# Attention decode over 16 heads: K and V loaded by pairs of heads, one head per 64 partitions, instead of head by head

## The chip, the core and the metric

The kernel runs on one NeuronCore of a Trainium2 chip. TensorE (PE) multiplies matrices into PSUM; VectorE (DVE), ScalarE (ACT) and GpSimdE (POOL) work element by element on SBUF, which has 128 partitions; the SyncE queue (SP) issues transfers, which 16 DMA engines carry out. Each engine runs its own program in order, and the programs meet only at semaphores. The metric is the device time of one execution in microseconds (us).

## The reference

One query per head against 8192 keys, with 16 heads of 256 numbers, in bf16:

```python
B, H, Sq, Sk, D = 1, 16, 1, 8192, 256
def reference(q, k, v):
    scale = q.shape[-1] ** -0.5
    scores = jnp.einsum("bhqd,bhkd->bhqk", q, k) * scale
    p = _softmax(scores, axis=-1)
    return jnp.einsum("bhqk,bhkd->bhqd", p, v)
```

K and V have 4 MB for each head, 134 MB together, and each byte is used once.

## The kernel before

**Layout.** A head's K lies on all 128 partitions: partition p holds the 64 keys 64p to 64p + 63 one behind the other, a row of 32 KB that is one contiguous run in memory. V lies alike. Two K buffers and two V buffers are used in turn.

**Loads.** SP issues all loads in the order of L16, 39 in all: the first head's K, the last head's K and the last three heads' V are cut (L15). K of head h waits until both engines that read K are through with head h - 2 (L121, L122), V of head h until the matmuls of head h - 2 are (L124). A transfer goes into its queue when its wait is over, behind those already there.

**Scores.** q of the head is copied to all partitions by a matmul into `qrow` (qcast, L244); ACT copies it to `q_now` in SBUF (q_copy, L347). A column is one key per partition. POOL multiplies the first 24 columns, four at a time, with `q_now` into one of two `prod` buffers (L184), and ACT sums each column into S (L396). DVE does the other 40 columns in four chunks of ten, product and sum in one instruction (L210). When all are in, DVE takes the maximum of each partition (m, L227).

**Softmax.** PE turns m into a row (L328), DVE takes its maximum (xmax, L199), PE spreads it over the partitions (L313), ACT negates it (L356) and makes the exponentials E and their sums (expo, L354). For head h this runs within the scores of head h + 1: xmax after DVE's first chunk, expo after ACT's second group.

**Output.** P·V is 32 matmuls, each on two columns with weights of 64 columns (doubles, L263); `collect` (L368) copies the two accumulators to SBUF, `gather` (L287) adds their parts up by four matmuls with selecting weights, `final` (L372) divides by the sum. PE's loop runs over h = 0 to 17, two rounds behind the scores. The last head's columns from 28 on go one by one, two matmuls each, straight to the output row (L330 to L342), so that only four columns are left when the last piece of V lands.

Of the kernel before, what the change touches and what calls it, by code (L numbers as in the profile page):

```python
# [5 lines left out]
ALU = mybir.AluOpType  # L6
# [4 lines left out]

NPL = 24
# [7 lines left out]
ROWS = 97  # L20
WIDE = BLK + 1
AHEAD = {"k1": 16, "kb": 16, "sp": 2, "pr": 1, "cm": 2, "pv": 1, "fin": 3, "rc": 3, "ex": 1, "mT": 1, "g": 1, "nb": 1}
STREAM_AHEAD = ("v0", "v1", "v0_40", "v1_48")


def bass_standalone__mha_softmax__decode_kernel(nc: bass.Bass, q: bass.AP, k: bass.AP, v: bass.AP, out: bass.AP):
# [15 lines left out]


    stream = []

    def load(kind, h):
        cuts = CUTS.get(f"{kind}{h}", (0,)) + (J,)
        for n, (a, b) in enumerate(zip(cuts, cuts[1:])):
            name = "kb" if kind == "k" and n else f"{kind}{h % 2}" + (f"_{a}" if n else "")
            stream.append((kind, h, a, b, name))  # L50

    for name in ORDER.split():
        load(name[0], int(name[1:]))

    with contextlib.ExitStack() as ctx:
# [16 lines left out]
        def back(h, n):  # L72

            if isinstance(h, int):
                return h - n
            return nc.s_assert_within(h - n, 0, H - 1, skip_runtime_bounds_check_because="the branch keeps it in range")
# [6 lines left out]
        S = sb("S", [P, H * J], FP32)  # L83
        E = sb("E", [P, 2 * EW], BF16)
        comb = sb("comb", [ROWS, 2 * D], FP32)
        sel = sb("sel", [ROWS, 2], FP32)
        m = sb("m", [P, 1], FP32)
        g = sb("g", [1, 1], FP32)
        negb = sb("negb", [P, 1], FP32)
        lsum = sb("lsum", [P, 1], FP32)  # L90
        recip = sb("recip", [WIDE, H], FP32)
        ident = sb("ident", [P, P], FP32)
        identb = sb("identb", [P, P], BF16)
        ones_row = sb("ones_row", [1, P], FP32)
        ones_col = sb("ones_col", [P, 1], FP32)
        o_all = sb("o_all", [1, H * D], out.dtype)

        acc = ps("acc", [P, 2 * D])
        ob = ps("ob", [P, 512])
# [6 lines left out]
        for name in ("pool", "cb", "cf", "ldq", "qp", "qb", "tp", "sp", "kd", "m", "mT", "g", "bc", "nb", "ex"):  # L106
            sem(name)
        for name in ("rc", "pr", "cm", "pv", "fin", "o"):
            sem(name)
        for _, _, _, _, name in stream:  # L110
            sem(name)

        def src(t, h):
            return t[0, h].rearrange("(p j) d -> p (j d)", p=P)

        @(lambda f: f(nc.sync))
        def _(sp):
            for kind, h, a, b, name in stream:
                if h >= 2 and a == 0:
                    if kind == "k":  # L120
                        sp.wait_ge(sem("kd"), (h - 1) * NC)  # L121
                        sp.wait_ge(sem("tp"), (h - 1) * NG)  # L122
                    else:
                        sp.wait_ge(sem("pr"), h + 2)  # L124
                buf = kbuf[:, h % 2 * J * D :] if kind == "k" else vbuf[h % 2]
                sp.dma_start(buf[:, a * D : b * D], src(k if kind == "k" else v, h)[:, a * D : b * D]).then_inc(  # L126
                    sem(name), 16
                )
            sp.wait_ge(sem(stream[-1][-1]), 16)
            sp.wait_ge(sem("fin"), LAST + 3)  # L130
            flat = out.rearrange("b h s d -> (b s) h d")
            rows = o_all[:, :].rearrange("s (h d) -> s h d", d=D)
            sp.dma_start(flat[:, 0:LAST, :], rows[:, 0:LAST, :]).then_inc(sem("o"), 16)
            sp.wait_ge(sem("fin"), H + 4)
            sp.dma_start(flat[:, LAST:H, :], rows[:, LAST:H, :]).then_inc(sem("o"), 16)
            sp.wait_ge(sem("o"), 32)
            sp.nop()
# [5 lines left out]

        @(lambda f: f(nc.gpsimd))
        def _(pool):
            def step(ins, n):
                ins.then_inc(sem("pool"), 1)
                pool.wait_ge(sem("pool"), n)

            def eye(t, n, done):  # L150
                step(pool.memset(t[:, :], 0.0), n)
                pool.affine_select(
                    out=t[:, :],
                    in_=t[:, :],
                    compare_op=ALU.not_equal,
                    fill=1.0,
                    base=0,
                    pattern=[[-1, P]],
                    channel_multiplier=1,
                ).then_inc(sem(done), 1)  # L160

            for name, n in AHEAD.items():
                pool.nop().then_inc(sem(name), n)
            for name in STREAM_AHEAD:
                pool.nop().then_inc(sem(name), 16)
            eye(identb, 1, "cb")
            eye(ident, 2, "cf")
            pool.memset(ones_row[:, :], 1.0).then_inc(sem("cf"), 1)
            pool.memset(ones_col[:, :], 1.0).then_inc(sem("cf"), 1)
            pool.memset(lsum[:, :], 0.0).then_inc(sem("cf"), 1)  # L170
            pool.memset(g[:, :], 0.0).then_inc(sem("cf"), 1)
            pool.memset(comb[:, :], 0.0).then_inc(sem("cf"), 1)
            step(pool.memset(sel[:, :], 0.0), 3)
            for n in range(4):
                step(pool.memset(sel[n * BLK : n * BLK + 1, n % 2 : n % 2 + 1], 1.0), n + 4)
            pool.memset(E[:, :], 0.0).then_inc(sem("cf"), 1)

            with pool.Fori(0, H) as h:
                par = pool.snap(h % 2)
                with pool.Fori(0, NG // 2) as i:  # L180
                    k_waits(pool, h)
                    for b in range(2):
                        pool.wait_ge(sem("sp"), h * NG + i * 2 + (b + 1))
                        pool.tensor_tensor(  # L184
                            out=prod[:, b * GRP * D : (b + 1) * GRP * D].rearrange("p (b d) -> p b d", b=GRP),
                            in0=kbuf[:, ds(par * (J * D) + i * (2 * GRP * D) + b * (GRP * D), GRP * D)].rearrange(
                                "p (b d) -> p b d", b=GRP
                            ),
                            in1=q_now[:, ds(par * D, D)].rearrange("p (b d) -> p b d", b=1).to_broadcast([P, GRP, D]),
                            op=ALU.mult,  # L190
                        ).then_inc(sem("tp"), 1)

        @(lambda f: f(nc.vector))
        def _(dve):
            def recips(h, n, after=0):
                dve.wait_ge(sem("pr"), h - n + (3 + after))
                dve.reciprocal(recip[:, ds(back(h, n), 1)], tot[0:WIDE, :]).then_inc(sem("rc"), 1)  # L197

            def xmax(h, n):  # L199
                dve.wait_ge(sem("mT"), h - n + 2)  # L200
                dve.tensor_reduce(g[:, :], mx[0:1, 0:P], AX.X, ALU.max).then_inc(sem("g"), 1)  # L201

            with dve.Fori(0, H) as h:
                par = dve.snap(h % 2)
                with dve.Fori(0, NC) as c:  # L205
                    k_waits(dve, h)
                    dve.wait_ge(sem("kb"), (h * 8 + c + 119) // 120 * 16 + 16)  # L207
                    for b in range(CH):
                        col = kbuf[:, ds(par * (J * D) + c * (CH * D) + (NPL + b) * D, D)]
                        ins = dve.scalar_tensor_tensor(  # L210
                            out=col,
                            in0=col,
                            scalar=SCALE,
                            in1=qrow[:, ds(par * 512, D)],
                            op0=ALU.mult,
                            op1=ALU.mult,
                            accum_out=S[:, ds(h * J + c * CH + (NPL + b), 1)],
                        )
                    ins.then_inc(sem("kd"), 1)
                    with dve.If(c == 0):  # L220
                        with dve.If(h > 1):
                            recips(h, 2)
                        with dve.If(h > 0):
                            xmax(h, 1)
# [18 lines left out]
        def _(pe):  # L243
# [19 lines left out]
            def doubles(par, a, b, waits):  # L263
                for j in range(a, b, 2):
                    if j in waits:
                        pe.wait_ge(*waits[j])
# [35 lines left out]
            for n in range(2):  # L302
                qcast(n, slice(n, n + 1))
# [142 lines left out]
```

## Time and profile before

| | |
|---|---|
| time, median of 3 runs | 318.48 us (318.28 to 318.66) |
| span of the profiled execution | 316.7 us |
| DVE busy | 232.5 us (73%) |
| POOL busy | 204.4 us (65%) |
| ACT busy | 197.9 us (62%) |
| PE busy | 141.7 us (45%), mean granted clock 0.752 |
| bytes read | 134.23 MB, 424 GB/s over the span |

The profile is one execution. The span runs from the first to the last instruction; the time has some 1.8 us more around it. Rows of the page's groups give line, engine, operation, output <- inputs, count, busy time and mean ns of one, then the engine's idle time just before and what ended most of it. Rows of the timeline give start and length in us, and idle time before in brackets with what released it. PEld is PE's loading of weights. An engine that is idle costs nothing by itself; what counts is which wait ends last.

### The profile page before, as it was taken

What the parts mean: (1) busy time and instruction counts of PE and PEld (TensorE: products, weight loads), DVE (VectorE), ACT (ScalarE), POOL (GpSimd) and SP (SyncE); (2) the same over time, 40 slices, a digit from 0 to 9 for tenths busy, and PEclk for the clock granted to TensorE, in tenths of its full rate; (3) what the DMA queues carried; (4) which work ended last, traced back from release to release, by engine and by line L of the source; (5) the groups of instructions that cost most, each with busy time, mean ns of one, the idle gap of its engine ahead of it and who ended that gap; (6) DMA issues with size and microseconds to landing.
All of it is one profiled execution on the core that took longest, in us unless ns stands there. A gap on an engine that the chain in (4) does not pass through costs nothing.

```text
span 316.7 us, 7915 instructions
## 1 busy us (share of the span) xinstructions
PE 141.7 (45%) x866; PEld 66.2 (21%) x866; DVE 232.5 (73%) x1329; ACT 197.9 (62%) x881; POOL 204.4 (65%) x115
## 2 busy tenths in 40 slices
PE   3101417253382642628282550715319064271977
PEld 1000103031130321204040220302113021130434
DVE  0797979497694967969797969769396793969800
ACT  2476737477374864768686857747386473968621
POOL 3788758395683857859687748568385783896500
PEclk9999999659576595857677595855857659585899
DMA  7999999999999999999999999999999999999996
GB/s 300 430 464 401 459 430 430 435 426 435 426 443 418 451 410 459 402 459 402 459 401 464 397 464 397 464 402 459 414 447 422 439 430 430 412 432 420 432 425 266
DMA packets 5653, 134.25 MB, mean 424 GB/s; under 512 B 642, under 2 KB 659, under 8 KB 916
## 3 DMA queue, kind: packets, MB, share of 16 engines
q1 hardware_dynamic: 5620, 134.23, 98.9%
q8 instruction: 1, 0.02, 0.0%
q10 hardware_dynamic: 32, 0.01, 0.0%
HBM read 134.23 MB, written 0.01 MB: 424 GB/s over the span
## 4 chain that ended last, share of the span: by engine, by line
DMA 59%; DVE 18%; issue 9%; DVEq 8%; PE 4%; SPq 0%; ACT 0%
DMA kbuf<-in_k_dram 35%; DMA vbuf<-in_v_dram 25%; DVE kbuf L210 18%; DVEq L210 5%; PE acc L268 4%; DVEq L207 1%; DVEq L205 1%; DVEq L142 1%; SPq L126 0%; PE ob L335 0%; DVEq L141 0%; DVE g L201 0%; DVE recip L197 0%; DVEq L225 0%; DVEq L197 0%
## 5 line engine op out<-in xcount | busy, mean ns | idle before, releaser
L210 DVE SCALAR_TENSOR_TENSOR kbuf<-kbuf,qrow x640 | 223.8, 417 | 52.6 <-issue 27.5
L184 POOL TENSOR_TENSOR prod<-kbuf,q_now 128x1024 f32 x96 | 201.9, 2124 | 90.1 <-DMA kbuf<-in_k_dram 59.0
L396 ACT ACTIVATE prod<-prod x384 | 154.5, 403 | 69.9 <-POOL prod L184 66.2
L268 PE MATMUL acc<-vbuf,E 128*64 128x512 bf16 x494 | 83.9, 513 | 30.7 <-DMA vbuf<-in_v_dram 30.1
L396 ACT ACTIVATION_READ_ACCUMULATOR prod<-prod x384 | 71.6, 186 | 0.0
L210 DVE DVE_READ_ACCUMULATOR kbuf<-kbuf,qrow x640 | 53.0, 83 | 0.0
L268 PEld LDWEIGHTS acc<-vbuf,E 128*64 128x64 bf16 x494 | 36.0, 146 | 72.3 <-issue 31.9
L313 PE MATMUL mx<-g,ones_row 1*128 1x1 f32 x34 | 9.7, 351 | 72.4 <-DVE g L201 72.3
L290 PE MATMUL ob<-comb,sel 97*1 97x128 f32 x144 | 14.2, 332 | 41.7 <-ACT comb L370 41.7
L350 ACT ACTIVATE q_now<-qrow (+1 forms) x17 | 6.5, 384 | 28.5 <-PE qrow L245 28.3
L313 PEld LDWEIGHTS mx<-g,ones_row 1*128 1x128 f32 x34 | 8.2, 298 | 76.9 <-DVE g L201 76.3
L279 PE MATMUL spare<-ident 128*128 128x512 f32 x36 | 22.2, 700 | 0.0
L290 PEld LDWEIGHTS ob<-comb,sel 97*1 97x1 f32 x144 | 5.6, 91 | 59.5 <-ACT comb L370 54.8
L328 PE MATMUL mx<-ident,m 128*1 128x128 f32 x32 | 8.1, 343 | 22.2 <-DVE m L227 22.2
L227 DVE TENSOR_REDUCE m<-S 128x1 f32 x16 | 3.5, 220 | 15.2 <-ACT prod L396 14.2
L370 ACT ACTIVATE comb<-acc 97x512 f32<-97x512 f32 x16 | 9.5, 596 | 6.1 <-PE tot L255 5.7
L359 ACT ACTIVATE E<-S,negb x16 | 9.3, 582 | 4.1 <-ACT negb L356 4.1
L377 ACT ACTIVATE o_all<-ob,recip 1x128 f32 x30 | 10.8, 359 | 1.5 <-PE ob L290 1.3
L197 DVE RECIPROCAL recip<-tot 33x1 f32 (+1 forms) x16 | 2.5, 155 | 10.2 <-PE tot L255 10.2
L328 PEld LDWEIGHTS mx<-ident,m 128*1 128x1 f32 x32 | 3.1, 100 | 24.6 <-DVE m L227 23.2
L245 PE MATMUL qrow<-q_sb,identb 16*128 16x256 bf16 x18 | 6.0, 347 | 4.7 <-DMA q_sb<-in_q_dram 4.7
L279 PEld LDWEIGHTS spare<-ident 128*128 128x128 f32 x36 | 5.8, 201 | 0.3
(27 smaller groups left out, 30.7 us busy)
## 6 DMA issues: line engine op xcount, KB each, us to landing
kbuf<-in_k_dram SPq DMA_DIRECT2D x14, 4096.0 KB, 21.1
vbuf<-in_v_dram SPq DMA_DIRECT2D x13, 4096.0 KB, 27.1
kbuf<-in_k_dram SPq DMA_DIRECT2D x2, 2176.0 KB, 13.3
kbuf<-in_k_dram SPq DMA_DIRECT2D x2, 1920.0 KB, 17.5
vbuf<-in_v_dram SPq DMA_DIRECT2D x1, 3072.0 KB, 29.9
vbuf<-in_v_dram SPq DMA_DIRECT2D x1, 2560.0 KB, 20.2
vbuf<-in_v_dram SPq DMA_DIRECT2D x1, 1792.0 KB, 11.1
vbuf<-in_v_dram SPq DMA_DIRECT2D x1, 1536.0 KB, 23.5
```

Of the source, the lines that this page charges most:

```text
L184: pool.tensor_tensor(out=prod[:, b * GRP * D : (b + 1) * GRP * D].rearrange("p (b d) -> p b d", b=GRP), in0=kbuf[:, ds(par * (J * D) + i * ...
L210: ins = dve.scalar_tensor_tensor(out=col, in0=col, scalar=SCALE, in1=qrow[:, ds(par * 512, D)], op0=ALU.mult, op1=ALU.mult, accum_out=S[:, ...
L268: ins = pe.matmul(acc[at : at + STRIP, :], lhsT=E[:, par * EW + j // 2 :][:, 0:STRIP], rhs=vbuf[par][:, j * D : (j + 2) * D], start=(j < 4 ...
L279: pe.matmul(spare[:, :].rearrange("p (b x) -> p b x", x=P), lhsT=ident[:, :], rhs=ident[:, :].rearrange("p (b x) -> p b x", b=1).to_broadc ...
L290: ins = pe.matmul(ob[row : row + 1, 0:HW], lhsT=sel[:, n : n + 1], rhs=comb[:, n * D + a : n * D + a + HW], start=(n == 0), stop=(n == 1), ...
L313: pe.matmul(sm, lhsT=ones_row[:, :], rhs=g[:, :], start=True, stop=True).then_inc(sem("bc"), 1)
L328: pe.matmul(mx[0:1, 0:P], lhsT=m[:, :], rhs=ident[:, :], start=True, stop=True).then_inc(sem("mT"), 1)
L350: act.activation(out=q_now[:, ds(par * D, D)], in_=qrow[:, ds(par * 512, D)], func=ACT.Copy).then_inc(sem("qb"), 1)
L359: act.activation(out=E[:, ds(i % 2 * EW, J)].rearrange("p (two x) -> p x two", two=2), in_=S[:, ds(i * J, J)].rearrange("p (x two) -> p x ...
L370: act.activation(out=comb[:, :], in_=acc[0:ROWS, :], func=ACT.Copy).then_inc(sem("cm"), 1)
L377: ins = act.activation(out=o_all[:, ds(i * D + a, HW)], in_=ob[row : row + 1, 0:HW], func=ACT.Copy, scale=recip[row : row + 1, ds(i, 1)],)
L396: ins = act.activation(out=part, in_=part, func=ACT.Copy, scale=SCALE, accum_out=S[:, ds(back(h, 0) * J + i * GRP + b, 1)],)
```

## The change

A load now brings K or V of two heads. Head 2n lies on partitions 0 to 63 and head 2n + 1 on partitions 64 to 127; a partition holds 128 keys, a run of 64 KB. There are eight pairs, 16 loads of 8 MB, five more by cuts, in all 21: only the last pair's K (two halves) and V (five pieces) are cut. There are two K buffers as before, of twice the size, but one V buffer; the last pair's V goes into the first K buffer. `q_now` is one buffer instead of two, and `q_copy` for the next pair comes after ACT's last group of this one. A pair has two sides of 64 columns; on each, POOL and ACT take 24 columns in groups of three (before: four) and DVE 40 in chunks of ten. Maximum, sum and result have two values, one for each head: `spread` makes two matmuls, `expo` two exponentials of 64 partitions each, interleaved with zeros in E so that one matmul serves both heads with different weights. `expo` comes after ACT's third group of the next pair, `collect` and `final` after its last. P·V runs in the round of the next pair; in the last round PE waits for the last pair's m before it starts the pair before. The last pair's columns from 92 on go one by one.

The diff, cut to its core:

```diff
-GRP = 4
+GRP = 3
-CUTS = {"k0": (0, 34), "k15": (0, 34), "v13": (0, 48), "v14": (0, 40), "v15": (0, 28, 48, 60)}
-ORDER = "k0 k1 v0 k2 v1 k3 v2 k4 v3 k5 v4 k6 k7 v5 k8 v6 k9 v7 k10 v8 k11 v9 k12 v10 k13 v11 k14 v12 k15 v13 v14 v15"
-LAST_PAIRED = 28
+SIDES = 2
+ORDER = "k0 k1 v0 k2 v1 k3 v2 k4 v3 k5 v4 k6 v5 k7 v6 v7"
+CUTS = {"k7": (0, 64), "v7": (0, 56, 92, 112, 124)}
+LAST_PAIRED = 92
...
+    NP = H // 2
+    HP = P // 2
+    J = Sk // HP
+    HJ = J // SIDES
...
+    NG = SIDES * NPL // GRP
+    SG = NPL // GRP
+    SC = (HJ - NPL) // CH
+    NC = SIDES * SC
...
-        vbuf = [sb(f"vbuf{i}", [P, J * D], dt) for i in range(2)]
-        q_sb = sb("q_sb", [H, D], dt)
-        q_now = sb("q_now", [P, 2 * D], dt)
+        vbuf = sb("vbuf", [P, J * D], dt)
+        q_now = sb("q_now", [P, D], dt)
...
+        def src(t, n):
+            return t[0, 2 * n : 2 * n + 2].rearrange("h (p j) d -> (h p) (j d)", p=HP)
...
+            for kind, n, a, b, name in stream:
+                if a == 0:
+                    if kind == "k" and n >= 2:
+                        sp.wait_ge(sem("kd"), (n - 1) * NC)
+                        sp.wait_ge(sem("tp"), (n - 1) * NG)
+                    elif kind == "v" and n == LAST:
+                        sp.wait_ge(sem("kd"), LAST * NC)
+                        sp.wait_ge(sem("tp"), LAST * NG)
+                    elif kind == "v" and n >= 1:
+                        sp.wait_ge(sem("pr"), n)
+                if kind == "k" and n == 1:
+                    sp.nop().then_inc(sem("k1"), 16)
+                    sp.nop().then_inc(sem("kb"), 16)
+                if kind == "k":
+                    buf = kbuf[:, n % 2 * J * D :]
+                else:
+                    buf = last_v if n == LAST else vbuf
+                sp.dma_start(buf[:, a * D : b * D], src(k if kind == "k" else v, n)[:, a * D : b * D]).then_inc(
                     sem(name), 16
                 )
...
+            with pool.Fori(0, NP) as h:
                 par = pool.snap(h % 2)
+                with pool.Fori(0, SIDES) as s:
+                    with pool.Fori(0, SG // 2) as i:
+                        k_waits(pool, h)
+                        side_wait(pool, h, s)
+                        for b in range(2):
+                            pool.wait_ge(sem("sp"), h * NG + s * SG + i * 2 + (b + 1))
+                            pool.tensor_tensor(
...
+            with dve.Fori(0, NP) as h:
                 par = dve.snap(h % 2)
+                with dve.Fori(0, SIDES) as s:
+                    with dve.Fori(0, SC) as c:
+                        k_waits(dve, h)
+                        side_wait(dve, h, s)
+                        for b in range(CH):
+                            col = kbuf[:, ds(par * (J * D) + s * (HJ * D) + c * (CH * D) + (NPL + b) * D, D)]
...
+                        ins.then_inc(sem("kd"), 1)
+                        with dve.If(c == 0):
+                            with dve.If(h > 0):
+                                with dve.If(s == 0):
+                                    xmax(h, 1)
+                                with dve.If(s == 1):
+                                    recips(h, 1)
...
+            def spread():
+                for n in range(2):
+                    ins = pe.matmul(
+                        sm[n * HP : (n + 1) * HP, :],
+                        lhsT=ones[0:1, :].to_broadcast([1, HP]),
+                        rhs=g[:, n : n + 1],
+                        start=True,
+                        stop=True,
+                    )
+                ins.then_inc(sem("bc"), 1)
...
+            with pe.Fori(0, NP) as h:
                 par = pe.snap(h % 2)
+                with pe.If(h > 0):
+                    pe.wait_ge(sem("g"), h)
+                    spread()
+                    pe.wait_ge(sem("ex"), h)
+                    total()
+                with pe.If(h == LAST):
+                    pe.wait_ge(sem("m"), NP)
+                    turned()
+                    pe.wait_ge(sem("g"), NP)
+                    spread()
+                with pe.If(h > 0):
+                    pe.wait_ge(sem("v"), h * 16)
+                    doubles(acc, 0, vbuf, 0, J).then_inc(sem("pr"), 1)
+                with pe.If(h < LAST):
+                    with pe.If(h > 0):
+                        keep_running()
+                        pe.wait_ge(sem("cm"), h)
+                        pe.wait_ge(sem("fin"), h)
+                        gather().then_inc(sem("pv"), 1)
                     pe.wait_ge(sem("m"), h + 1)
-                    pe.matmul(mx[0:1, 0:P], lhsT=m[:, :], rhs=ident[:, :], start=True, stop=True).then_inc(sem("mT"), 1)
-                    qcast(par, ds(h + 2, 1))
+                    turned()
+                    with pe.If(h < NP - 2):
+                        qcast(back(h, -2), par)
+            cuts = CUTS["v7"]
+            e = EW
+            pe.wait_ge(sem("ex"), NP)
+            total()
+            doubles(acc_last, e, last_v, 0, cuts[1], cuts, LAST_PAIRED)
+            pe.wait_ge(sem("cm"), LAST)
+            pe.wait_ge(sem("fin"), LAST)
+            gather().then_inc(sem("pv"), 1)
+            doubles(acc_last, e, last_v, cuts[1], LAST_PAIRED, cuts, LAST_PAIRED).then_inc(sem("pr"), 1)
+            keep_running()
+            pe.wait_ge(sem("cm"), NP)
+            pe.wait_ge(sem("fin"), NP)
+            gather()
...
+                    pe.wait_ge(sem(f"w{j}"), 16)
+                at = e + pos(j)
...
+            def q_copy(n, at):
+                act.wait_ge(sem("qp"), n + 1)
+                act.activation(out=q_now[:, :], in_=qrow[:, ds(at * 512, D)], func=ACT.Copy).then_inc(sem("qb"), 1)
...
+                at = EW if h is NP else 0
+                for x in range(2):
+                    rows = slice(x * HP, (x + 1) * HP)
+                    ins = act.activation(
+                        out=E[rows, at : at + 2 * J].rearrange(
+                            "p (b two i t) -> p b i two t", b=J // BLK, two=2, t=2
+                        )[:, :, :, :, x],
+                        in_=S[rows, ds(i % 2 * J, J)].rearrange("p (b i two) -> p b i two", b=J // BLK, two=2),
+                        func=ACT.Exp,
+                        bias=negb[rows, :],
+                        scale=1.0,
+                        accum_out=lsum[rows, :],
+                    )
+                ins.then_inc(sem("ex"), 1)
...
+            with act.Fori(0, NP) as h:
+                par = act.snap(h % 2)
+                other = act.snap((h + 1) % 2)
+                with act.Fori(0, SIDES) as s:
+                    with act.Fori(0, SG) as i:
+                        act.wait_ge(sem("tp"), h * NG + s * SG + i + 1)
...
                         with act.If(h > 0):
+                            with act.If(s == 0):
+                                with act.If(i == 2):
+                                    expo(h, 1)
+                with act.If(h < LAST):
+                    q_copy(h + 1, other)
+                    with act.If(h > 0):
+                        collect(h, 1, acc)
+                        final(h, 1)
+            expo(NP, 1)
+            collect(LAST, 1, acc)
+            final(LAST, 1)
+            collect(NP, 1, acc_last)
```

More of the change, by code (lines that the diff above doesn't have):

```diff
@@ L129, in _ @@
             sp.wait_ge(sem(stream[-1][-1]), 16)
+            sp.wait_ge(sem("fin"), LAST + 1)
+            flat = out.rearrange("b (n two) s d -> two (b n s) d", two=2)
+            rows = qo[:, :].rearrange("t (n d) -> t n d", d=D)
+            sp.dma_start(flat[:, 0:LAST, :], rows[:, 0:LAST, :]).then_inc(sem("o"), 16)
             sp.wait_ge(sem("fin"), LAST + 3)
[L131 to L135, printed above, removed]
+            sp.dma_start(flat[:, LAST:NP, :], rows[:, LAST:NP, :]).then_inc(sem("o"), 16)
             sp.wait_ge(sem("o"), 32)
@@ L172, in _ @@
[L172 to L178, printed above, removed]
-                par = pool.snap(h % 2)
[L180 to L191, printed above, removed]
+            step(pool.memset(ident[:, :], 0.0))
@@ new lines, in _ @@
+            keep(ident, 0, 1, -1, ALU.not_equal, 1.0)
+            step(pool.memset(ones, 1.0))
+            step(pool.memset(half[:, :], 1.0))
+            for c in (0, BLK):
+                step(pool.memset(half[HP:P, c : c + 1], 0.0))
+                step(pool.memset(half[0:HP, c + 1 : c + 2], 0.0))
+            step(pool.memset(E[:, :], 0.0))
+            for c in range(2):
+                step(
+                    pool.tensor_tensor(
+                        out=sel[:, 2 * c : 2 * c + 2],
+                        in0=ident[0:ROWS, c * BLK : c * BLK + 2],
+                        in1=ident[0:ROWS, STRIP + c * BLK : STRIP + c * BLK + 2],
+                        op=ALU.add,
+                    )
+                )
@@ L203, in _ @@
-            with dve.Fori(0, H) as h:
-                par = dve.snap(h % 2)
[L205 to L224, printed above, removed]
+                dve.wait_ge(sem("mT"), h - n + 1)
@@ L233, in _ @@
+            recips(NP, 1)
+            dve.wait_ge(sem("pv"), NP + 1)
+            dve.wait_ge(sem("rc"), NP)
             row, a = halves[1]
             dve.tensor_scalar(
-                out=o_all[:, LAST * D + a : LAST * D + a + HW],
-                in0=ob[row : row + 1, 0:HW],
-                scalar1=recip[0:1, LAST:H],
+                out=qo[:, LAST * D + a : LAST * D + a + HW],
+                in0=ob[row : row + 2, 0:HW],
+                scalar1=recip[row : row + 2, LAST:NP],
                 scalar2=None,
@@ L251, in qcast, with turned, total, doubles @@
                 ).then_inc(sem("qp"), 1)
-            def total(h):
-                pe.wait_ge(sem("ex"), (h * H + 2 * H + 1) // (H + 1))
+            def turned():
+                pe.matmul(mx[0:1, 0:P], lhsT=m[:, :], rhs=ident[:, :], start=True, stop=True).then_inc(sem("mT"), 1)
+            def spread():
[6 more added lines that the diff above has]
+                        stop=True,
+                    )
+                ins.then_inc(sem("bc"), 1)
+            def total():
                 pe.matmul(
-                    tot[0:WIDE, :],
-                    lhsT=lsum[:, :].to_broadcast([P, WIDE]),
-                    rhs=ones_col[:, :],
+                    tot[0 : BLK + 2, :],
+                    lhsT=half[:, :],
+                    rhs=lsum[:, :],
                     start=True,
                     stop=True,
-                ).then_inc(sem("pr"), 1)
-            def doubles(par, a, b, waits):
+                ).then_inc(sem("tt"), 1)
+            def doubles(to, e, buf, a, b, waits=(), last=J):
                 for j in range(a, b, 2):
                     if j in waits:
-                        pe.wait_ge(*waits[j])
+                        pe.wait_ge(sem(f"w{j}"), 16)
                     at = j // 2 % 2 * STRIP
+                    x = pos(j)
                     ins = pe.matmul(
-                        acc[at : at + STRIP, :],
-                        lhsT=E[:, par * EW + j // 2 :][:, 0:STRIP],
-                        rhs=vbuf[par][:, j * D : (j + 2) * D],
+                        to[at : at + STRIP, :],
+                        lhsT=E[:, e + x : e + x + STRIP],
+                        rhs=buf[:, j * D : (j + 2) * D],
                         start=(j < 4),
-                        stop=(j >= J - 4),
+                        stop=(j >= last - 4),
                         skip_group_check=True,
@@ L290, in gather @@
                         ins = pe.matmul(
[L291 to L292 removed]
+                            ob[row : row + 2, 0:HW],
+                            lhsT=sel[:, 2 * n : 2 * n + 2],
                             rhs=comb[:, n * D + a : n * D + a + HW],
@@ L342, in _ @@
                     )
[L343 removed]
+            ins.then_inc(sem("pv"), 2)
         @(lambda f: f(nc.scalar))
         def _(act):
[L347 to L352 removed]
+            def q_copy(n, at):
+                act.wait_ge(sem("qp"), n + 1)
+                act.activation(out=q_now[:, :], in_=qrow[:, ds(at * 512, D)], func=ACT.Copy).then_inc(sem("qb"), 1)
@@ L368, in collect @@
-            def collect(h, n):
-                act.wait_ge(sem("pr"), h - n + 4)
-                act.activation(out=comb[:, :], in_=acc[0:ROWS, :], func=ACT.Copy).then_inc(sem("cm"), 1)
+                at = EW if h is NP else 0
[10 more added lines that the diff above has]
+                        accum_out=lsum[rows, :],
+                    )
@@ L372, in final, with collect @@
+                ins.then_inc(sem("ex"), 1)
+            def collect(h, n, frm):
+                act.wait_ge(sem("pr"), h - n + 1)
+                act.activation(out=comb[:, :], in_=frm[0:ROWS, :], func=ACT.Copy).then_inc(sem("cm"), 1)
             def final(h, n):
-                act.wait_ge(sem("pv"), h - n + 4)
-                act.wait_ge(sem("rc"), h - n + 4)
+                act.wait_ge(sem("pv"), h - n + 1)
+                act.wait_ge(sem("rc"), h - n + 1)
                 i = back(h, n)
@@ L400, in _ @@
                                 scale=SCALE,
-                                accum_out=S[:, ds(back(h, 0) * J + i * GRP + b, 1)],
+                                accum_out=S[:, ds(par * J + s * HJ + i * GRP + b, 1)],
                             )
                         ins.then_inc(sem("sp"), 1)
-                    with act.If(i == 1):
                         with act.If(h > 0):
-                            with act.If(h < H + 1):
-                                expo(h, 1)
-                        with act.If(h > 2):
-                            final(h, 3)
-                with act.If(h > 1):
-                    collect(h, 2)
-            act.wait_ge(sem("pv"), H + 4)
-            act.wait_ge(sem("rc"), H + 3)
-            act.activation(out=o_all[:, LAST * D : LAST * D + HW], in_=ob[0:1, 0:HW], func=ACT.Copy, scale=recip[0:1, LAST:H]).then_inc(
+                            with act.If(s == 0):
[10 more added lines that the diff above has]
+            collect(NP, 1, acc_last)
+            act.wait_ge(sem("pv"), NP + 1)
+            act.wait_ge(sem("rc"), NP)
+            act.activation(out=qo[:, LAST * D : LAST * D + HW], in_=ob[0:2, 0:HW], func=ACT.Copy, scale=recip[0:2, LAST:NP]).then_inc(
                 sem("fin"), 1
```

230 lines of the change are left out of this document (94 added, 136 removed).

## The prediction, made before the changed kernel was timed

> **What bounds the kernel now.** I read the span, the DMA row and the costliest groups on the page first, then the busy time by windows, the PE timeline, and last the end of the timeline.
>
> ```profile
> span 316.7 us, 7915 instructions
> q1 hardware_dynamic: 5620, 134.23, 98.9%
> L210 DVE SCALAR_TENSOR_TENSOR kbuf<-kbuf,qrow x640 | 223.8, 417 | 52.6 <-issue 27.5
> L184 POOL TENSOR_TENSOR prod<-kbuf,q_now 128x1024 f32 x96 | 201.9, 2124 | 90.1 <-DMA kbuf<-in_k_dram 59.0
> ```
> ```profile
> 24.00:260.00 236.00, 105.19 (x581) 48.50 (x583) 187.12 (x1073) 155.02 (x702) 162.50 (x78) 0.71 1.00 432
> 294.00:313.00 19.00, 15.76 (x142) 7.71 (x138) 5.65 (x32) 7.18 (x26) 2.90 (x2) 0.95 1.01 427
> ```
>
> The 16 DMA engines are busy for 98.9% of 316.7, or 313 us; every compute engine idles in between. The loads are the bound, and only what the tail adds behind the last byte counts besides. The windows (span and length, then busy PE, PEld, DVE, ACT, POOL, the clock, DMA share, GB/s) show a full DMA share throughout: 432 GB/s with whole 32 KB rows and 427 where the last heads come in pieces of 2 to 20 KB. The stream has a steady beat, seen in PE's blocks of 32 paired matmuls (start, length), of which those from 236.57 to 275.43 were released by a landed V:
>
> ```profile
> 143.25 4.92 PE L268 MATMUL acc<-vbuf,E 128*64 128x512 bf16 x32 [0.17 <-issue]
> ...
> 236.57 6.04 PE L268 MATMUL acc<-vbuf,E 128*64 128x512 bf16 x32 [4.31 <-DMA vbuf<-in_v_dram]
> 256.00 6.56 PE L268 MATMUL acc<-vbuf,E 128*64 128x512 bf16 x32 [4.46 <-DMA vbuf<-in_v_dram]
> 275.43 5.39 PE L268 MATMUL acc<-vbuf,E 128*64 128x512 bf16 x32 [4.31 <-DMA vbuf<-in_v_dram]
> 301.24 2.35 PE L268 MATMUL acc<-vbuf,E 128*64 128x512 bf16 x20
> 309.09 1.70 PE L268 MATMUL acc<-vbuf,E 128*64 128x512 bf16 x14 [1.18 <-DMA vbuf<-in_v_dram]
> ```
>
> Two 4 MB loads take 19.43 us (236.57 to 256.00), which is one load of a pair. The end, in order:
>
> ```profile
> 299.21 0.22 DVE L227 TENSOR_REDUCE m<-S 128x1 f32 x1 [0.26 <-DVE kbuf L210]
> 311.09 0.60 ACT L370 ACTIVATE comb<-acc 97x512 f32<-97x512 f32 x1 [2.06 <-PE tot L255]
> 312.25 1.15 PEld L335 LDWEIGHTS ob<-vbuf,E 128*1 128x1 bf16 x40
> 314.06 1.06 PE L335 MATMUL ob<-vbuf,E 128*1 128x128 bf16 x32 [0.48 <-DMA vbuf<-in_v_dram]
> 315.16 0.36 ACT L414 ACTIVATE o_all<-ob,recip 1x128 bf16<-1x128 f32 x1 [3.47 <-PE ob L335]
> ```
>
> The last scores are complete at 299.2, 15 us before the last V columns arrive at 314.06, so the softmax and most of P·V hide under the stream. The span ends 1.5 us after L414 starts, and the time shown, 318.48, is 1.8 us more than the span.
>
> **The loads.** Bytes are the same, so long runs gain only what a row costs beside its bytes. From 427 to 432 is 1.2% between rows of about 10 KB (mean of the last pieces) and 32 KB. If that is a fixed cost per row, f/10 - f/32 = 1.2% gives f = 0.17 KB, and 64 KB instead of 32 KB saves 0.17/64 = 0.3%: 0.8 us over the stream, 0.6 by pair 6. Ends: nothing if the 64 KB row is cut in two, 1.2% (3.7 us) if the pieces' whole loss is repeated; I take 0.8, nearest to the row of whole loads. [...]
>
> **Do the buffers keep the stream full?** K of pair 0 lands after two 4 MB loads. V10 (in the order of L16 the 24th load of 4 MB) was seen at 236.57, so byte for byte K0 is there at 236.57 - 11 x 19.43 = 22.8, V0 at 61.7. Pair 0 takes DVE and POOL some 29 to 30 us (below), to 53; K2 has to be issued before V0 ends at 61.7: 8 us to spare. V_n needs the one V buffer: V5 is in at 256.0, its 64 matmuls take 9 (below), and V6's turn comes at 275.4: 10 us to spare. So the stream runs through; V7 has landed at about 313, as V15 does now.
>
> **What no longer hides: the scores.** K lies in units twice as long, whole until pair 7 (only k7 is cut), and the last 40 us of stream are V6 and V7. K6 is the 12th of 16 loads, so it lands when V10 does: 236.6 - 0.6 = 236.0. Then pairs 6 and 7 are scored, one behind the other.
>
> ```profile
> 266.42 4.20 POOL L184 TENSOR_TENSOR prod<-kbuf,q_now 128x1024 f32 x2 [5.45 <-DMA kbuf<-in_k_dram]
> 268.80 0.42 ACT L396 ACTIVATE prod<-prod  x1 [3.52 <-POOL prod L184]
> 270.98 4.20 POOL L184 TENSOR_TENSOR prod<-kbuf,q_now 128x1024 f32 x2 [0.36 <-issue]
> 284.46 0.39 ACT L350 ACTIVATE q_now<-qrow  x1 [1.34 <-PE qrow L245]
> 285.03 0.42 ACT L396 ACTIVATE prod<-prod  x1 [0.18 <-issue]
> 286.55 0.19 ACT L396 ACTIVATION_READ_ACCUMULATOR prod<-prod  x1
> 287.20 4.20 POOL L184 TENSOR_TENSOR prod<-kbuf,q_now 128x1024 f32 x2 [1.80 <-ACT prod L396]
> 288.84 0.17 ACT L356 ACTIVATE negb<-mx 128x1 f32<-128x1 f32 x1 [0.51 <-PE mx L313]
> 289.27 0.58 ACT L359 ACTIVATE E<-S,negb  x1 [0.26 <-ACT negb L356]
> 289.63 0.73 ACT L377 ACTIVATE o_all<-ob,recip 1x128 f32 x2
> ```
> ```profile
> 8.15 1.02 PE L290 MATMUL ob<-comb,sel 97*1 97x128 f32 x8
> ```
>
> POOL and ACT form a chain through two prod buffers. A POOL group of 4 columns takes 2.12; of 3 columns 1.6 (by size; it lies between 1.59 and the 2.12 of today). ACT starts 0.27 after POOL ends (266.42 + 2.12 to 268.80) and takes 1.7 for four columns (285.03 to 286.74), 1.3 for three. POOL needs 0.46 to see a freed buffer (286.74 to 287.20) and 0.36 for its loop. Two groups thus take 2 x 1.6 + 0.36 = 3.56 by POOL alone, 1.6 + 0.27 + 1.3 + 0.46 = 3.63 around a buffer: I take 3.6. A pair has 48 such columns, 16 groups, 8 rounds: 28.8, less the first 0.36, plus ACT's last 1.57.
>
> expo is now in ACT's path after the third group: 0.43 from negb to the exponential, then two of about 0.65 (the row's 0.58, with 64 more elements in each row): 1.8. ACT's later groups free POOL's buffers, so POOL stalls: group 2 is done at 6.7 from POOL's start, expo until 8.5, group 3 until 9.8, POOL goes on at 10.3 instead of 8.8: 1.5. **Pair 6** takes 28.8 - 0.36 + 1.57 + 1.5 = 31.5. POOL starts 0.7 after PE would see the landing (K14 fell midway between 256.00 and 275.43, at 265.7; POOL began at 266.42): 236.7 + 31.5 = 268.2.
>
> **Pair 7** can't start before: q_now is one buffer, and q_copy comes after ACT's last group. POOL starts 1.0 later (0.1 + 0.39 + 0.46). But behind q_copy ACT now runs collect (0.60), waits for gather, cold at 1.02, and runs final (0.73); then its loop jumps back, 1.34 before L350 today. ACT's first group starts 4.4 after the end of pair 6. The rounds follow: ACT's groups 0 and 1 end at 5.7 and 7.0, POOL's groups 2 and 3 at 7.8 and 9.4, ACT's group 2 at 9.4, expo at 11.3, ACT's group 3 at 12.6, POOL's groups 5 and 6 start at 13.1 and 15.1; five more rounds (18.0 - 0.36) and ACT's 1.57 make 34.3. The scores are complete at 268.2 + 34.3 = 302.5, and m starts 0.3 later: **302.8, against 299.2 now**. If the jumps of the new loop over sides cost like the one below, it is up to 3 us more; I take nothing, as POOL's 0.36 is nearest.
>
> DVE beside it:
>
> ```profile
> 16.58 0.33 DVE kbuf L210
> 20.18 0.33 DVE kbuf L210
> ```
> ```profile
> 170.04 0.22 DVE L227 TENSOR_REDUCE m<-S 128x1 f32 x1 [0.26 <-DVE kbuf L210]
> 171.79 0.42 DVE L210 SCALAR_TENSOR_TENSOR kbuf<-kbuf,qrow  x1 [1.53 <-issue]
> 266.72 0.42 DVE L210 SCALAR_TENSOR_TENSOR kbuf<-kbuf,qrow  x1 [3.41 <-issue]
> ```
>
> Ten columns repeat every 3.60 (16.58, 20.18): a pair is 28.8. Even if DVE alone set the pace, it starts at 236.0 + 1.0 (265.7 to 266.72), has two pairs of 28.8 with 2.0 between (m's wait 0.26 and 170.04 to 171.79), and m starts at 296.9. That is the floor.
>
> **The tail from m (M).** PE's order in its last round is: wait for pair 7's m, turned, spread, and only then pair 6's 64 matmuls, although V6 has been there since 294; V7's come behind them, and nothing hides any of it.
> - M to the first matmul: now 299.21 to 301.24, 2.0; with a second spread 2.1.
> - 64 matmuls: warm they cost (2.35 - 1.70)/6 = 0.108 each; blocks of 32 after idling took 4.92 to 6.56, 5.39 at 275.43, or 1.9 more than 32 x 0.108. 64 x 0.108 + 1.9 = 8.8; I take 9.0 (8.4 to 10). They end at M + 11.1.
> - total 0.4, 28 matmuls of V7 3.0, gather 0.45, 18 matmuls 1.9, drain 0.3: M + 17.2. V7 has landed by then. collect of pair 6 and final run beside this.
> - collect of pair 7 to the first single: 311.09 to 312.25 now, so M + 18.4. keep_running is beside it.
> - 72 singles at 1.15/40 = 0.029, and 0.2: M + 20.7. L414 and the end, 1.5: M + 22.2.
>
> 302.8 + 22.2 = 325.0, and 1.8 outside: **326.8, say 327**. [...]
>
> **The rivals.**
> - *Tail hidden (faster, 4%).* One point decides: M at or before 292. Then M + 22 falls on the last landing, the stream alone decides, and it gives 318.5 - 0.8 = 317.7. For it: 0.8 gained, DVE idle 52.6 today. Against it: two pairs would need 27.5 us each, and DVE's floor is 28.8. DVE's floor itself, M at 296.9, gives 296.9 + 22.2 + 1.8 = 320.9; that is the forecast's low end.
> - *The stream breaks (8%).* q is now read as rows of two partitions beside K0's long rows; if it, the late first K or the one V buffer costs more than the 8 to 10 us to spare, each further us moves everything: 330 to 340. Against it: the sums above.
> - *Slower rows (8%).* The pitch from partition to partition doubles to 64 KB. Were the rate 3% lower for it (two and a half times the largest difference between the windows), K6 would come 7 us later and M with it: 334. No row has any other pitch than 32 KB; the equal rates of whole and cut rows speak against it. [...]
> - *Not one run of 64 KB* but two of 32: inside the forecast, 0.6 to 0.8 us more.
>
> **How the numbers follow.** The forecast has 80%: 320.9 (DVE's floor) to 331 (3 us of jumps, 1 of cold matmuls). Beyond lie the two slow rivals; to leave out no more than 2 in 10 the range is 320.5 to 332, which loses the fast rival and most of the broken stream. A measurement tells 0.2% from no change: faster 4%, within 2%, slower 94%.
>
> **What would show it.** DMA share near full to about 313, with gaps only if a buffer was late; a rate of 432 to 434 GB/s; POOL groups at 1.6 and rounds at 3.6; m of the last pair at 302.8; V6's block of 64 starting 2 us after it and not at its landing at 294; then PE busy without a wait for DMA to 323. The forecast is wrong if m comes before 297, if the 64 run before m, or if DMA idles in the middle.

## The result, and the profile after

| | before | after |
|---|---|---|
| time, median | 318.56 us (318.28 to 318.66, 4 runs) | 326.57 us (324.94 to 326.67, 4 runs) |
| ratio after / before | | 1.0242, 95% interval 1.022 to 1.0264 |
| span of the profiled execution | 316.7 us | 325.3 us |

The changed kernel is 2.4% slower; the medians lie 8.0 us apart. (Of the kernel with rows of 32 KB further down, one run, 328.18 us at a granted clock of 0.623 against 0.731 to 0.748 of its others, is in a slower state and left out.) In what follows K6 is K of pair 6, V6 its V, and the singles are the 72 matmuls on one column each at the end. The page of its profile, the lines that answer to those of before:

```profile
span 325.3 us, 7432 instructions
...
q1 hardware_dynamic: 3044, 134.23, 95.7%
q8 instruction: 2, 0.03, 0.0%
...
L244 DVE SCALAR_TENSOR_TENSOR kbuf<-kbuf,qrow x640 | 223.8, 417 | 62.1 <-issue 56.1
L215 POOL TENSOR_TENSOR prod<-kbuf,q_now 128x768 f32<-128x768 bf16 x128 | 207.8, 1640 | 89.1 <-DMA kbuf<-in_k_dram 43.1
```

The packets are fewer (3044, of 5620) and longer. Their time is 95.7% of 325.3, or 311.3 us, against 313.2 before: the loads themselves got shorter. The span has grown past their end. Windows of after (span and length, busy PE, PEld, DVE, ACT, POOL, then clock, DMA share, GB/s):

```profile
24.00:260.00 236.00, 68.48 (x442) 30.86 (x444) 191.71 (x1095) 157.30 (x690) 174.29 (x108) 0.71 1.00 433
312.00:315.00 3.00, 3.00 (x34) 1.76 (x30) 0.16 (x1) 0.57 (x1) 0.00 (x0) 1.00 0.20 78
314.00:317.00 3.00, 3.00 (x32) 2.37 (x30) 0.16 (x1) 0.60 (x1) 0.00 (x0) 1.00 0.01 3
```

The share is 1.00 in the middle, so the one V buffer and the whole first K break nothing. After 314 nothing is loaded any more, and PE is busy throughout. The end in the timeline of after (start, length, in brackets the idle time before and its releaser):

```profile
303.64 0.29 DVE L262 TENSOR_REDUCE small<-S 128x1 f32 x1 [1.43 <-ACT prod L460]
305.24 9.14 PE L316 MATMUL acc<-vbuf,E 128*64 128x512 bf16 x64
314.28 3.19 PE L316 MATMUL acc_last<-kbuf,E 128*64 128x512 bf16 x27
317.94 2.13 PE L316 MATMUL acc_last<-kbuf,E 128*64 128x512 bf16 x18
320.11 0.60 ACT L434 ACTIVATE comb<-acc_last 98x512 f32<-98x512 f32 x1 [1.33 <-PE acc_last L316]
321.49 2.18 PE L396 MATMUL ob<-kbuf,E 128*2 128x128 bf16 x72
323.71 0.36 ACT L483 ACTIVATE qo<-ob,small 2x128 bf16<-2x128 f32 x1 [3.00 <-PE ob L396]
```

The last m comes at 303.64 (299.21 before). Pair 6's 64 matmuls start behind it, at 305.24, and none of the rows up to 321.49 waits for a DMA. Where the two pairs ahead of it spend their time, in the timeline of POOL and of ACT:

```profile
237.71 3.23 POOL L215 TENSOR_TENSOR prod<-kbuf,q_now 128x768 f32<-128x768 bf16 x2 [8.33 <-DMA kbuf<-in_k_dram]
241.44 3.23 POOL L215 TENSOR_TENSOR prod<-kbuf,q_now 128x768 f32<-128x768 bf16 x2 [0.51 <-ACT prod L460]
...
248.43 3.23 POOL L215 TENSOR_TENSOR prod<-kbuf,q_now 128x768 f32<-128x768 bf16 x2 [1.62 <-ACT prod L460]
...
271.26 3.23 POOL L215 TENSOR_TENSOR prod<-kbuf,q_now 128x768 f32<-128x768 bf16 x2 [3.04 <-issue]
```
```profile
269.82 0.36 ACT L410 ACTIVATE q_now<-qrow 128x256 bf16 x1
270.09 0.58 ACT L434 ACTIVATE comb<-acc 98x512 f32<-98x512 f32 x1
271.57 0.73 ACT L441 ACTIVATE qo<-ob,small 2x128 f32 x2 [0.90 <-PE ob L338]
273.29 0.42 ACT L460 ACTIVATE prod<-prod  x1 [0.99 <-POOL prod L215]
```

POOL waits 8.33 us for pair 6's K and starts at 237.71; a round of two groups takes 3.73 (237.71 to 241.44), expo stalls POOL for 1.62, and pair 7 starts only behind q_copy (269.82), which fills the one `q_now` anew after ACT's last group, 33.55 us after pair 6.

### The profile page after: what moved, and what is told of

Same layout as the page of the kernel before. It is cut to its first block, busy times and chain, and to the rows that moved or that the text cites. A ratio compares the mean times of both kernels' runs of the same rounds, so it can differ in the third digit from the quotient of the medians.

```text
span 325.3 us, 7432 instructions
## 1 busy us (share of the span) xinstructions
PE 96.9 (30%) x716; PEld 45.7 (14%) x716; DVE 229.2 (70%) x1305; ACT 194.7 (60%) x840; POOL 210.8 (65%) x146
## 3 DMA queue, kind: packets, MB, share of 16 engines
q1 hardware_dynamic: 3044, 134.23, 95.7%
## 4 chain that ended last, share of the span: by engine, by line
DMA 33%; POOL 19%; ACT 13%; issue 11%; ACTq 7%; PE 6%; DVE 5%; POOLq 3%; DVEq 3%; SPq 0%
DMA kbuf<-in_k_dram 33%; POOL prod L215 19%; ACT prod L460 11%; ACTq L460 5%; DVE kbuf L244 5%; PE acc L316 3%; POOLq L215 2%; PE acc_last L316 2%; DVEq L244 2%; ACTq L456 1%; ACT E L420 1%; PE ob L396 1%; POOLq L214 1%; PE ob L338 0%; PE spare L327 0%
## 5 line engine op out<-in xcount | busy, mean ns | idle before, releaser
L215 POOL TENSOR_TENSOR prod<-kbuf,q_now 128x768 f32<-128x768 bf16 x128 | 207.8, 1640 | 89.1 <-DMA kbuf<-in_k_dram 43.1
L316 PE MATMUL acc<-vbuf,E 128*64 128x512 bf16 x448 | 64.7, 460 | 37.0 <-DMA vbuf<-in_v_dram 36.8
L316 PEld LDWEIGHTS acc<-vbuf,E 128*64 128x64 bf16 x448 | 29.6, 132 | 69.3 <-DMA vbuf<-in_v_dram 37.2
L288 PE MATMUL mx<-ident,small 128*1 128x128 f32 x16 | 4.7, 395 | 75.5 <-DVE small L262 75.5
L338 PE MATMUL ob<-comb,small 98*2 98x128 f32 x64 | 6.9, 356 | 41.9 <-ACT comb L434 41.9
L420 ACT ACTIVATE E<-S,negb 64x128 bf16 (+1 forms) x16 | 13.8, 863 | 1.4 <-ACT negb L414 1.2
L441 ACT ACTIVATE qo<-ob,small 2x128 f32 (+1 forms) x14 | 5.0, 359 | 10.5 <-PE ob L338 10.4
L434 ACT ACTIVATE comb<-acc 98x512 f32<-98x512 f32 x7 | 4.1, 584 | 7.2 <-PE acc L316 7.2
L327 PE MATMUL spare<-ident 128*128 128x512 f32 x14 | 7.9, 645 | 0.0
L420 ACT ACTIVATION_READ_ACCUMULATOR E<-S,negb 64x1 f32 x16 | 7.9, 492 | 0.0
```

The source lines that it names most:

```text
L215: pool.tensor_tensor(out=prod[:, b * GRP * D : (b + 1) * GRP * D].rearrange("p (b d) -> p b d", b=GRP), in0=kbuf[:, ds(par * (J * D) + s * ...
L288: pe.matmul(mx[0:1, 0:P], lhsT=m[:, :], rhs=ident[:, :], start=True, stop=True).then_inc(sem("mT"), 1)
L316: ins = pe.matmul(to[at : at + STRIP, :], lhsT=E[:, e + x : e + x + STRIP], rhs=buf[:, j * D : (j + 2) * D], start=(j < 4), stop=(j >= las ...
L327: pe.matmul(spare[:, :].rearrange("p (b x) -> p b x", x=P), lhsT=ident[:, :], rhs=ident[:, :].rearrange("p (b x) -> p b x", b=1).to_broadc ...
L338: ins = pe.matmul(ob[row : row + 2, 0:HW], lhsT=sel[:, 2 * n : 2 * n + 2], rhs=comb[:, n * D + a : n * D + a + HW], start=(n == 0), stop=( ...
L420: ins = act.activation(out=E[rows, at : at + 2 * J].rearrange("p (b two i t) -> p b i two t", b=J // BLK, two=2, t=2)[:, :, :, :, x], in_= ...
```

## The experiments

The theory to test: the time is lost behind the last m. It comes late because pairs 6 and 7 are scored one behind the other from K6's landing on, and PE's order keeps pair 6's matmuls behind it. The rivals: only the lateness of the scores counts; pair 7's own K sets it; the loads (long rows, one V buffer) are slower. Each kernel is the changed one with the edit named.

**Pair 6's matmuls ahead of the wait for m.** In PE's loop the block for the last round goes behind the matmuls:

```diff
+                with pe.If(h > 0):
+                    pe.wait_ge(sem("v"), h * 16)
+                    doubles(acc, 0, vbuf, 0, J).then_inc(sem("pr"), 1)
                 with pe.If(h == LAST):
                     pe.wait_ge(sem("m"), NP)
...
-                with pe.If(h > 0):
-                    pe.wait_ge(sem("v"), h * 16)
-                    doubles(acc, 0, vbuf, 0, J).then_inc(sem("pr"), 1)
```

> The changed kernel, but in PE's last round pair 6's 64 matmuls stand ahead of the wait for pair 7's m. Theory (late scores, and PE's order holds pair 6's matmuls behind them): they start when V6 lands, at 295, and end at 304; m stays at 303.6; from there only turned, spread, expo and pair 7's 46 matmuls and 72 singles are left, so the last single ends at 316.7 instead of 323.7: time 319.6 (319 to 320.5). Rival A (only the lateness of the scores costs, the 64 matmuls are hidden anyway): 326.6. Rival B (the longer rows or the one V buffer cost the time in the loads): 326.6, with last landing unchanged.

Measured: 321.08 us (318.91 to 321.8, 7 runs), 1.0061 of before (1.0035 to 1.0087): 5.5 us of the 8 are back. m from DVE's timeline, then PE's:

```profile
302.45 0.28 DVE L262 TENSOR_REDUCE small<-S 128x1 f32 x1 [1.43 <-ACT prod L460]
294.92 9.56 PE L316 MATMUL acc<-vbuf,E 128*64 128x512 bf16 x64 [15.32 <-DMA vbuf<-in_v_dram]
304.40 0.38 PE L288 MATMUL mx<-ident,small 128*1 128x128 f32 x2
307.58 4.46 PE L316 MATMUL acc_last<-kbuf,E 128*64 128x512 bf16 x27
316.06 2.18 PE L396 MATMUL ob<-kbuf,E 128*2 128x128 bf16 x72
```

The 64 start with the landing of V6, 10.3 us earlier than after. Both rivals fall: they had 326.6. The expectation had m at 303.6; it came at 302.45, and `turned`, the matmul that turns m into a row, waits for PE until 304.40, so m is no longer what decides. The size was 1.5 us short of what the theory said, and the row of 27 matmuls has most of it: they took 3.19 after and 4.46 here. The seven times fall into two groups: three of 318.91 to 319.76, about as expected, with a mean granted clock of 0.737, and four of 321.08 to 321.80, with 0.728 to 0.733; the trace is of one of the four. Between 304.4 and 307.4 PE has little to do, and the granted clock went down in this execution, from 0.91 in the window of 304.00 to 307.40 to 0.61 behind it; in that of the third experiment, with the same pause, it stayed at 1.00 (windows behind the pause, of the first and of the third; the clock is the third figure from the end):

```profile
307.40:311.00 3.60, 3.56 (x23) 2.56 (x25) 0.16 (x1) 0.60 (x1) 0.00 (x0) 0.61 0.99 414
```
```profile
307.40:310.60 3.20, 3.17 (x30) 2.20 (x30) 0.16 (x1) 0.60 (x1) 0.00 (x0) 1.00 0.98 410
```

**Pair 6's K in halves.** PE's order as in the changed kernel:

```diff
-CUTS = {"k7": (0, 64), "v7": (0, 56, 92, 112, 124)}
+CUTS = {"k6": (0, 64), "k7": (0, 64), "v7": (0, 56, 92, 112, 124)}
...
-            e.wait_ge(sem("kb"), (h * SIDES + s + 1) // (NP * SIDES) * 16 + 16)
+            e.wait_ge(sem("kb"), (h * SIDES + s + 3) // (NP * SIDES) * 16 + 16)
+            e.wait_ge(sem("kc"), (h * SIDES + s + 1) // (NP * SIDES) * 16 + 16)
```

> The changed kernel, but pair 6's K comes in two halves, as pair 7's does; PE's order unchanged. Theory (the last two pairs are scored one behind the other, and the start of pair 6 is its K landing whole at 236.3): pair 6 starts when pair 5 is done, about 231.2 instead of 237.7, and m of pair 7 comes at 297.2 instead of 303.6; as everything behind m follows it, time 320.2 (319.5 to 321). Rival A (pair 7's own K sets m: it lands at 264.8 and 275.7): m and the time stay, 326.6. Rival B (the loads): 326.6.

Measured: 322.62 us (321.67 to 323.4, 4 runs), 1.0123 of before (1.0106 to 1.0139): 4.0 us back, with pair 7's K and PE's order as they were. From the timelines of POOL, DVE and PE:

```profile
233.55 3.23 POOL L217 TENSOR_TENSOR prod<-kbuf,q_now 128x768 f32<-128x768 bf16 x2 [3.21 <-issue]
267.67 3.23 POOL L217 TENSOR_TENSOR prod<-kbuf,q_now 128x768 f32<-128x768 bf16 x2 [3.62 <-DMA kbuf<-in_k_dram]
```
```profile
300.06 0.29 DVE L264 TENSOR_REDUCE small<-S 128x1 f32 x1 [0.57 <-ACT prod L462]
301.67 9.52 PE L318 MATMUL acc<-vbuf,E 128*64 128x512 bf16 x64
318.29 2.18 PE L398 MATMUL ob<-kbuf,E 128*2 128x128 bf16 x72
```

Pair 6 follows pair 5 without a wait for its K, 4.2 us earlier than after; m comes 3.6 earlier, and the singles 3.2. What follows m follows it but for 0.4, by which the 64 matmuls took longer (9.52 against 9.14), and rival A falls for the changed kernel. It is not far off, though: pair 7 (the second row) now waits for the first half of its own K, whose last packet comes at 266.23, and starts 34.1 behind pair 6 instead of 33.55; that is where 0.6 of the 4.2 stayed. By this row a still earlier pair 6 would gain nothing (not run). The time is 2.4 above the expected 320.2, as m is 2.9 behind its 297.2: the expectation had pair 6 at 231.2 and pair 7 without a wait. Most of the 2.3 us by which pair 6 is behind it is K5's lateness, which goes with the instruction packet of the last section (at 129.2 here, at 269.4 in the third experiment): there K5 landed 1.5 earlier, and pair 6 starts at 231.90. The other 0.7 is open.

**Both.**

> e1 and e2 together. Theory: the two do not add up. m comes at 297.2, but PE is busy with pair 6's 64 matmuls from V6's landing at 295 until 304, so turned, spread and expo wait for them: E at 307.5, end of the singles 317, time 319.5 to 320. If the two gains were independent it would be 313.5, which is under what the stream of loads allows; if only the loads counted, 318.

Measured: 320.81 us (319.73 to 322.16, 4 runs), 1.009 of before (1.0059 to 1.0121), no better than the first alone. The four times split like those of the first, 319.73 and 319.74 at a mean granted clock of 0.737, 321.88 and 322.16 at 0.728 and 0.729, so no run is near the median; the trace is of the first of them. The rows of m and of `turned`:

```profile
298.43 0.28 DVE L264 TENSOR_REDUCE small<-S 128x1 f32 x1 [0.58 <-ACT prod L462]
304.39 0.38 PE L290 MATMUL mx<-ident,small 128*1 128x128 f32 x2
```

m is 5.2 us earlier than after, and `turned`, which reads it, comes 6.0 later still: PE is at V6's matmuls until then. The gains do not add up, as expected; with m early, the lateness of V6 as a whole is next.

**V of pair 6 in halves, too.** The edit: `"v6": (0, 64)` in CUTS, and PE waits for the second half by itself:

```diff
-                    doubles(acc, 0, vbuf, 0, J).then_inc(sem("pr"), 1)
+                    doubles(acc, 0, vbuf, 0, HJ)
+                    pe.wait_ge(sem("vb"), h // LAST * 16 + 16)
+                    doubles(acc, 0, vbuf, HJ, J).then_inc(sem("pr"), 1)
```

> e3, and V of pair 6 in two halves, the second 32 of its matmuls behind a wait of their own. Theory: the first 32 run at 285, the second 32 at 295 to 300, m at 297.2, E at 304, pair 7's matmuls with the landing of V7's pieces; the end is the last landing, 314, and some 2.6 us as before the change: time 317.5 to 318.5, no slower than the kernel before, and up to 0.3% faster if the 64 KB rows keep their rate. Rival (one engine of the DMA is late at the end, or the single V buffer holds up the stream): 319 or more, with the last landing after 315.

Measured: 318.51 us (318.12 to 319.04, 11 runs), 1.0007 of before (0.9998 to 1.0016), and in a second set 318.30, 1.0001 (0.9992 to 1.001). PE's timeline of the first set:

```profile
285.56 5.65 PE L319 MATMUL acc<-vbuf,E 128*64 128x512 bf16 x32 [10.29 <-DMA vbuf<-in_v_dram]
295.27 5.33 PE L319 MATMUL acc<-vbuf,E 128*64 128x512 bf16 x32 [4.06 <-DMA vbuf<-in_v_dram]
303.78 4.65 PE L319 MATMUL acc_last<-kbuf,E 128*64 128x512 bf16 x28
312.86 2.44 PE L401 MATMUL ob<-kbuf,E 128*2 128x128 bf16 x72
```

The singles begin at 312.86, before the last piece lands (its last packet comes at 314.4), and the whole loss is gone with two cuts and one moved block; the pairs, the one V buffer and the long rows of the first six pairs are all still there. It doesn't beat the kernel before.

**Rows of 32 KB.** That kernel with every whole load cut at column 64, compared with it in one set:

```diff
-CUTS = {"k6": (0, 64), "k7": (0, 64), "v6": (0, 64), "v7": (0, 56, 92, 112, 124)}
+CUTS = {f"k{n}": (0, 64) for n in range(6)} | {f"v{n}": (0, 64) for n in range(6)} | {"k6": (0, 64), "k7": (0, 64), "v6": (0, 64), "v7": (0, 56, 92, 112, 124)}
```

> The kernel of e5_v6_cut_too once more, beside the two others of this set: 318.0 to 318.8, last landing at 314.4, 1.7 us between the first and the last of the 16 engines in the last pieces.

> e5 with every load of 8 MB cut in two halves of 64 columns, so that no run is longer than 32 KB; work and waits are the same. Theory (64 KB rows carry 0.4% more, but one engine that loads instructions in the middle of the stream falls 1 us behind and lands last, which takes the gain back): the stream's beat is 19.43 us for 8 MB instead of 19.35, the same engine is late all the same, and the last landing moves from 314.4 to about 315.5: time 319.5 (319.0 to 320.0). Rival A (long rows gain nothing): 318.5. Rival B (the late engine is late because its packets are 64 KB long, so short rows lose less to it): 317.8 to 318.3.

Measured: 318.98 us (11 runs), 1.0024 of before (1.0014 to 1.0034), against 318.30 with the long rows: the long rows of those twelve loads are worth 0.7 us. The blocks of PE that wait for V show the beat, first with 64 KB, then with 32 KB:

```profile
138.84 9.75 PE L319 MATMUL acc<-vbuf,E 128*64 128x512 bf16 x64 [5.64 <-DMA vbuf<-in_v_dram]
177.54 9.18 PE L319 MATMUL acc<-vbuf,E 128*64 128x512 bf16 x64 [8.78 <-DMA vbuf<-in_v_dram]
```
```profile
217.12 9.32 PE L321 MATMUL acc<-vbuf,E 128*64 128x512 bf16 x64 [8.97 <-DMA vbuf<-in_v_dram]
255.98 8.67 PE L321 MATMUL acc<-vbuf,E 128*64 128x512 bf16 x64 [14.10 <-DMA vbuf<-in_v_dram]
```

Two loads of 8 MB take 38.70 against 38.86 us: 0.4%. Both rivals fall, the one that gave the long rows nothing and the one that blamed them for the late landing: the gap of the last section grows from 0.39 to 1.72 us with 64 KB and with 32 KB.

**Fewer singles** (`LAST_PAIRED = 112` instead of 92 in the kernel with the three edits).

> e5 with pair 7's columns one by one from 112 on instead of 92, so that PE's program has 60 instructions less and 32 singles instead of 72. If the 16 KB of instructions that come in the middle of the stream are PE's tail and a shorter tail does without them, all 16 engines end together, the last landing is at 313.0 and the time 317.0 to 317.5; if not, the last landing stays at 314.4 and the time at 318.0 to 318.9, since the collect of pair 7 then ends near the last landing, too.

Measured: 319.26 us (8 runs), 1.0034 of before (1.0022 to 1.0046). A 16 KB packet of the instruction queue still comes in the middle of the stream, at 272.5, and the last landing is at 314.3, so the hope behind it failed. The time is above the other forecast, too (318.0 to 318.9). The profiled execution, span 320.8, had a lower granted clock than the others (0.654 on average, against 0.736 in that of the kernel without this edit). The seven others had 0.731 to 0.747, like the kernel without it, and their median is 319.06, so the edit costs some 0.8 us; where, this trace of another clock can't tell.

## Why the prediction was right

It said 327 and was 0.4 us off, by the mechanism that it named. That it came so near is in part luck: m came 0.8 later than forecast, and the tail and the time outside of the span were 0.5 shorter each. Point by point, predicted and measured:

| step | predicted | after |
|---|---|---|
| two 8 MB loads, by long rows 0.3% less than 38.86 | 38.74 | 38.70 |
| POOL starts pair 6 | 236.7 | 237.71 |
| POOL: group, round of two, stall by expo | 1.6, 3.6, 1.5 | 1.64, 3.73, 1.62 |
| pair 6's start to pair 7's | 32.5 | 33.55 |
| pair 7's start to m | 33.6 | 32.4 |
| m | 302.8 | 303.64 |
| m to the first of the 64 | 2.1 | 1.6 |
| the 64 matmuls | 9.0 | 9.0 (305.24 to 314.22) |
| from there to the first single | 7.3 | 7.3 (314.22 to 321.49) |
| first single to the end | 3.8 | 3.8 |
| outside of the span | 1.8 | 1.3 |

- **The bound and where it goes.** Right: the stream stays full, and the time is m plus a tail of 21.7 (predicted 22.2). The second experiment shows that tail as nearly constant (300.06 to a span of 322.1: 22.0), the first that PE's order is what makes it so long, and the fourth that nothing of the loss is left once K6 and V6 come in halves as well.
- **The start of pair 6.** 1.0 late. Rate and bytes were right, but behind 94.5 the last of a load's 16 small packets came 1.1 us further behind the first (0.64 to 1.77; last section): K6's last packet came at 236.31, and at 235.19 in the first experiment, where this begins only at 273.5. The same lag took back what the long rows gained: of the 16 last small packets of V7, all but two were there by 312.9, and the last at 314.06; before, the last two of V15 came at 314.06 and 314.22. So the prediction's "about 313, as V15 does now" misread its own row at 314.06; V7's landing is no term of its sum.
- **The two pairs.** The sum was right, 65.9 against 66.1, with errors that cancel. A plain round costs 0.13 more than taken, so q_copy came 32.1 behind the start of pair 6 and not 31.6, and POOL started 1.1 after q_copy was done, where 0.46 was taken. But ACT did not pay 1.34 for its loop's jump: final ends at 272.30, and ACT then waits 0.99 for POOL (the row at 273.29). Those 1.34 before L350 in the kernel before were read as the jump; the trace named PE as the releaser.
- **The engines' share.** The range's low end was DVE's own pace. After, m waits 1.43 for ACT: POOL and ACT set the pace, as forecast, and DVE was through with its part 1.4 sooner.
- **Rivals.** The hidden tail needed m by 292, and m was 303.64. The stream did not break: DMA share 1.00. The doubled pitch cost nothing that shows: 433 GB/s from 24 to 260, against 432 before. The rows do go as single runs: of the 3044 packets 1792 are of 64 KB, 2.43 us each.

## What to carry to other kernels

When a change makes the units of a stream larger, the steady state may not notice, but the last two units do: work out when the last unit's chain ends with nothing behind it, and cut the last units (whether cutting the first would help, no run shows). In an engine's program in order, look for the wait that stands ahead of work that is ready; moving 64 ready matmuls ahead of one wait was worth more here (5.5 us) than cutting a load (4.0), and it took a second cut besides both to win all of it back. A stream at 433 GB/s gained 0.4% in its beat from doubling runs of 32 KB, 0.7 us of the time, which is little beside a tail of 22 us.

## What the runs showed of the hardware

**A load's landings spread as a packet of the instruction queue passes.** For each load the trace has 16 small packets of 4 bytes, as many as there are DMA engines; the gap, worked out from the trace's packets, is the time between the first and the last of them. That each engine ends its part with one is the author's reading: the trace does not name the engine of a packet. Beside it the times at which a 16 KB packet of the instruction queue (the q8 line of the page) began and how long it took (a second such packet, at 323.3 in the changed kernel, comes behind the loads):

```
kernel              gap, from -> to                 loads that end at     instruction packet
before              0.49 to 0.51                    -                      313.7 (1.10 us), the stream's end
after               0.64 -> 1.77 us                 79.8 and 99.1          94.5 (0.99 us)
pair 6's K cut      0.39 -> 1.87 us                 119.1 and 138.5        129.2 (0.98 us)
three edits         0.39 -> 1.72 us                 263.9 and 273.6        270.1 (1.07 us)
rows of 32 KB       0.39 -> 1.72 us                 264.8 and 274.5        269.8 (1.06 us)
```

The other three kernels show the same, the first experiment (0.70 -> 1.80, packet at 273.5), the third (0.48 -> 1.99, at 269.4) and that with fewer singles (0.62 -> 1.88, at 272.5). Each time the gap grows by 1.1 to 1.5 us as the packet passes, and it stays: in after it is 1.70 to 1.86 from 99.1 to 311.5. That one engine carried the packet and is last from there on was not shown. The blocks of PE that wait for V tell it too: after has them at 101.37 and 140.07, 1.23 us behind the same loads at 100.14 and 138.84 in the second set of the kernel with three edits, whose packet comes at 270.

```profile
101.37 8.69 PE L316 MATMUL acc<-vbuf,E 128*64 128x512 bf16 x64 [2.33 <-DMA vbuf<-in_v_dram]
140.07 9.80 PE L316 MATMUL acc<-vbuf,E 128*64 128x512 bf16 x64 [7.48 <-DMA vbuf<-in_v_dram]
```
```profile
100.14 8.63 PE L319 MATMUL acc<-vbuf,E 128*64 128x512 bf16 x64 [0.65 <-DMA vbuf<-in_v_dram]
```

So these landings of V come 1.2 us later in after. That the packet causes the gap is inferred from the times in these eight kernels; whose instructions they are, and why the time differs so between kernels, stays open.

**Behind 3 us with little work for PE, the granted clock was 0.61 in one execution and 1.00 in another.** The first is that of the first experiment (PE busy for 1.06 us of the window of 304.00 to 307.40), the second that of the third (0.65 us of 304.40 to 307.40). They are one case of each; whether the pause lowers the clock, they do not show.
